# Half-width transposes without a copy ahead of them, a reordered first batch, and channel products placed between theta products, in a windowed attention with a phase-mixing layer

## The chip, the cores and the metric

The kernel runs on one core of a Trainium2 chip. The metric is the device time of one execution in microseconds, measured over several runs. A core has a matrix engine (PE; its weight loads are listed as PEld), a vector engine (DVE, VectorE), an activation engine (ACT, ScalarE), a general engine (POOL, GpSimd), a synchronisation engine (SP) and sixteen DMA engines. Each engine works through its own instructions in order; SP, ACT and POOL also issue transfers.

## The reference

Four batches, eight heads of 64, 768 tokens, float32. First an attention in which a token sees the 96 tokens up to itself and the first 8 tokens, with a bias that falls with distance:

```python
scores = scale * np.matmul(q, k.transpose(0, 1, 3, 2))
is_global = pos[None, :] < int(n_global)              # 8
is_local = (rel >= 0) & (rel < int(n_local))          # 96
bias = -slopes[:, None, None] * dist[None, :, :]
a = softmax(np.where(is_global | is_local, scores + bias, -1e9))
x = np.matmul(a, v)                                   # heads side by side: 768 x 512
```

Then a layer in which tokens are mixed by two 768 x 768 matrices:

```python
theta = x @ w_theta
zr, zi = x * np.cos(theta), x * np.sin(theta)
u = x + w_tok_r @ zr + w_tok_i @ zi
out = u + np.maximum(u @ w_ch, 0.0)
```

## The kernel before

Tokens are tiled by 128, so a batch has NT = 6 token tiles; channels by 128, NC = 4; heads go in NP = 4 pairs, one pair filling 128 partitions with two heads of 64. Matrix work is in bf16.

**Loads.** POOL's queue loads and converts everything but the first head pair of batch 0, which comes as float32 through SP and ACT (L99) and is converted by the engines. `load_qk` (L70) gives each partition p the six consecutive tokens 6p to 6p+5 of each head; `load_v` (L86) has tokens by tile. The order on POOL is: Q and K of batch 0's pair 1, V's first half, pairs 2 and 3, V's second half, the weights (`load_w`, L154), then Q, K and V of batch 1, Q and K of batch 2, and later the rest.

**Transposed Q and K.** The scores need Q and K with the head dimension on partitions. For batches 0, 1 and 2 VectorE first copies a pair of heads from the loaded layout (head, token, 64) into `qkn`, laid out (token, head, 64): `cast0` (L193) for batch 0, `prep_copy` (L224) for batches 1 and 2. Then PE transposes six blocks of 128 x 128 into a PSUM tile (`turn0` L200, `prep` L232), and an engine copies the tile to `qT` or `kT` (`out0` L206; L249 on VectorE, L251 on ScalarE). `kglob` (L214) builds `kG`, K's tiles with their first 8 columns replaced by the 8 global tokens. Batch 3 is transposed by DMA instead (`prep_dma`, L256).

**Attention.** For a pair and a chunk of two key tiles, `score_mms` (L279) fills a PSUM tile: a matmul has 64 rows, and the two heads lie in the two halves of the rows. `score_exp` (L298) is one exponential on ScalarE. In batch 0 the bias is added by a matmul with a scaled identity (`score_bias`, L270); in the others VectorE multiplies by a table `etab` that ScalarE makes (`bias_table`, L140). `vglob` (L325) builds V's counterpart of kG, `values` (L336) multiplies by V and normalises into `x_sb`, and `xtrans` (L364) transposes a pair of x, by PE in batch 0 and by DMA later.

**The layer.** `theta` (L378) takes two token tiles; it has two steps, j = 0 (channel tiles 0 to 2 of the first token tile) and j = 1 (the rest, then cos and sin on ScalarE, L395, and the products zri on VectorE, L398). Channel tile 3 comes last, since it needs the last head pair. `mix` (L403) is the token mixing, `utrans` (L418) transposes u, `chan` (L430) makes the channel product, the output tile `o_sb` (L440) and its store (L442). `trans_w` (L164) transposes the mixing matrices.

**Order.** Batch 0's attention and theta are in an order written out by hand, from L510 to L574: three pairs are in flight, transposes are two pairs ahead, values one behind. From L580 on, `weave` (L488) traces the mixing of batch b as main work, with the preparation and attention of batch b+1 and the preparation of b+2 woven in by weights, and a scheduler settles each engine's final order. Before the mixing of batch b stand its theta steps `th` and the last three channel products of the batch before, `rest`, in the order of L587:

```python
order = th[:4] + rest[:2] + th[4:] + rest[2:] if b else []
```

PSUM has two large tiles, for scores, values and theta, and four small ones (`ps_small`) for all else.

Of the kernel before, what the change touches and what calls it, by code (L numbers as in the profile page):

```python
# [9 lines left out]
FP = mybir.dt.float32  # L10
# [6 lines left out]
def kernel(  # L17
# [13 lines left out]
    nc = tc.nc  # L31
# [76 lines left out]
    load_qk(0, 2, 2)  # L108
    load_v(0, 0, 4)
    load_qk(0, 4, 2)  # L110
# [29 lines left out]
    def bias_table(p):  # L140
        for h in (2 * p, 2 * p + 1):
            nc.scalar.activation(etab[:, h], dist[:, 0:5], AF.Exp, scale=-slopes[h])
# [50 lines left out]
    def cast0(p, i_, eng, h=None):  # L193
        if (p, "n") not in tiles0:
            tiles0[p, "n"] = att.tile([T, NT, 2, 2, D], BF, name="qkn", bufs=2)
        src = qk32[:, i_] if p == 0 else loads[0][0][:, i_, 2 * p:2 * p + 2]
        hs = slice(0, 2) if h is None else slice(h, h + 1)
        eng(out=tiles0[p, "n"][:, :, i_, hs].rearrange("p t h d -> p h t d"), in_=src[:, hs])

    def turn0(p, i_):  # L200
        qkn = tiles0[p, "n"]
        ps = tiles0[p, i_] = ps_small([T, NT, T], BF)
        for t_ in range(NT):
            nc.tensor.transpose(ps[:, t_, :], qkn[:, t_, i_].rearrange("p h d -> p (h d)"), ident)
# [9 lines left out]
    def kglob(b, p):  # L214
        kT = qkT[(b, p)][1]
        kG = qkT[(b, p)][2] = att.tile([T, NT - 2, T], BF, name="kG", bufs=6)
        with behind("dve") if b == B - 1 else nullcontext():
            nc.vector.tensor_copy(
                out=kG, in_=kT[:, T:(NT - 1) * T].rearrange("p (t n) -> p t n", t=NT - 2))
            nc.vector.tensor_copy(out=kG[:, :, 0:NG], in_=kT[:, None, 0:NG].to_broadcast([T, NT - 2, NG]))  # L220

    qkns = {}

    def prep_copy(b, p):  # L224
        qk = loads[b][0]
        qkn = qkns[b, p] = att.tile([T, NT, 2, 2, D], BF, name="qkn", bufs=2)
        with behind("dve"):
            for i_ in range(2):
                nc.vector.tensor_copy(  # L229
                    out=qkn[:, :, i_].rearrange("p t h d -> p h t d"), in_=qk[:, i_, 2 * p:2 * p + 2])  # L230

    def prep(b, p):  # L232
        if p == 0:
            prep_copy(b, 0)
        if p + 1 < NP:
            prep_copy(b, p + 1)
        qkn = qkns[b, p]
        qT = att.tile([T, S], BF, name="qT", bufs=6)
        kT = att.tile([T, S], BF, name="kT", bufs=6)
        for i_, dst in ((0, qT), (1, kT)):  # L240
            ps = ps_small([T, NT, T], BF)
            with behind("pe"):
                for t_ in range(NT):
                    nc.tensor.transpose(ps[:, t_, :], qkn[:, t_, i_].rearrange("p h d -> p (h d)"), ident)  # L244

            dst = dst.rearrange("p (n t) -> p n t", t=NT)
            src = ps.rearrange("p t n -> p n t")
            if i_ == 0:
                nc.vector.tensor_copy(out=dst, in_=src)  # L249
            else:  # L250
                nc.scalar.copy(out=dst, in_=src)  # L251

        qkT[(b, p)] = [qT, kT, None]
        kglob(b, p)
# [42 lines left out]

    def score_exp(b, p, c):  # L298
        e_t, pb = ebuf[(b, p)], pbs[b, p, c]
        n = min(4, 2 * NT - 1 - 4 * c) * T  # L300
        e_c = e_t[:, :, 2 * c:2 * c + 2].rearrange("p a j s n -> p a (j s n)")[:, :, 0:n]
        ins = nc.scalar.activation(e_c, pb[:, :, 0:n], AF.Exp, scale=scale).ins  # L302
        if c == NT // 2 - 1 and p == NP - 1:

            with tc.issue_after(ins) if b else nullcontext():
                nc.scalar.activation(junk, halfpi, AF.Sin)
        if b == 0:
            return
        tab = etab[:, 2 * p:2 * p + 2]
        if c == 0 or n < 4 * T:  # L310
            s0 = 0 if c == 0 else 2
            nc.vector.tensor_mul(e_c, e_c, tab[:, :, s0:s0 + n // T].rearrange("p a s n -> p a (s n)"))  # L312
        else:
            e4 = e_t[:, :, 2 * c:2 * c + 2].rearrange("p a j s n -> p a j (s n)")
            nc.vector.tensor_mul(  # L315
                e4, e4, tab[:, :, 2:4].rearrange("p a s n -> p a (s n)")[:, :, None, :].to_broadcast(
                    [T, 2, 2, 2 * T]))
# [18 lines left out]
    def values(b, p, hh):  # L336
        vn = loads[b][1]
        e_t, vG = ebuf[(b, p)], vGs[b]
        h = 2 * p + hh
        if b == 0:  # L340
            po = ps_small([T, 1, 512], FP)
        else:
            if hh == 0:
                pos[(b, p)] = ps_big()
            po = pos[(b, p)][:, hh:hh + 1, :]
        for it in range(NT):
            mms = [(e_t[:, hh, it, 0, :], vn[:, h, it, :])]
            if it:
                mms.append((e_t[:, hh, it - 1, 1, :], vG[:, h, it - 2, :] if it > 1 else vn[:, h, 0, :]))
            o = po[:, 0, it * (D + 1):(it + 1) * (D + 1)]  # L350
            for i_, (l_, r_) in enumerate(mms):
                nc.tensor.matmul(o, lhsT=l_, rhs=r_, start=(i_ == 0), stop=(i_ == len(mms) - 1))  # L352
        if b and hh == 0:
            return
        if b:
            po = pos[(b, p)]
        h0, n = (hh, 1) if b == 0 else (0, 2)
        po4 = po[:, :, 0:NT * (D + 1)].rearrange("p a (t d) -> p a t d", d=D + 1)
        rec = att.tile([T, n, NT, 1], FP, name="rec", tag=f"rec{n}")
        nc.vector.reciprocal(rec, po4[:, :, :, D:D + 1])  # L360
        xv = x_sb[b][:, p, :, h0 * D:(h0 + n) * D].rearrange("p t (a d) -> p a t d", a=n)
        nc.vector.tensor_mul(xv, po4[:, :, :, 0:D], rec.to_broadcast([T, n, NT, D]))  # L362

    def xtrans(b, p, copy=nc.vector.tensor_copy):  # L364
# [6 lines left out]
        for st in range(NT):  # L371
            nc.tensor.transpose(ps[:, st * T:(st + 1) * T], x_sb[b][:, p, st, :], ident)
        copy(out=xT_sb[b][:, p, :], in_=ps)
# [4 lines left out]
    def theta(b, c, j):  # L378
        if c == 0 and j == 0:
# [3 lines left out]
        if j == 0:  # L383
            pss["th"] = [ps_small([T, DM], FP) for _ in range(2)] if last else ps_big()
        pb = pss["th"]
        st = lambda j_: slice((2 * c + j_) * T, (2 * c + j_ + 1) * T)
        for j_, dc in ([(0, dc) for dc in range(NC - 1)] if j == 0 else
                       [(1, dc) for dc in range(NC - 1)] + [(0, NC - 1), (1, NC - 1)]):
            nc.tensor.matmul(pb[j_] if last else pb[:, j_, :], lhsT=xT[:, dc, st(j_)],  # L389
                             rhs=w_theta_bf[:, dc, :], start=(dc == 0), stop=(dc == NC - 1))  # L390
        if j == 1:
# [26 lines left out]
    def utrans(b, tt):  # L418
# [3 lines left out]
        if b and (b, tt) != (B - 1, NT - 1):  # L422
# [7 lines left out]
    def chan(b, tt):  # L430
        u, uT = u_sb[b, tt], uTs[(b, tt)]
        ps_c = ps_small([T, DM], FP)
        for dc in range(NC):
            nc.tensor.matmul(ps_c, lhsT=uT[:, dc, :], rhs=w_ch_bf[:, dc, :],  # L434
                             start=(dc == 0), stop=(dc == NC - 1))
        o_sb = moe.tile([T, DM], FP, name="o_sb", bufs=4)
        parts = 2 if (b, tt) == (B - 1, NT - 1) else 1
        for i_ in range(parts):
            cols = slice(i_ * DM // parts, (i_ + 1) * DM // parts)
            nc.vector.scalar_tensor_tensor(o_sb[:, cols], in0=ps_c[:, cols], scalar=0.0, in1=u[:, cols],  # L440
# [72 lines left out]
    cast0(0, 1, dve, 0)  # L513
    cast0(0, 1, act, 1)
    turn0(0, 1)
    cast0(0, 0, dve, 0)
    cast0(0, 0, act, 1)
    turn0(0, 0)
    out0(0, 1, act, 0)
# [3 lines left out]
    kglob(0, 0)  # L523
    score_bias(0, 0)
    score_bias(0, 1)
    score_mms(0, 0, 0)
    score_mms(0, 0, 1)
    score_exp(0, 0, 0)
    cast0(1, 1, dve)
    cast0(1, 0, dve)  # L530
    diagonals(1)
    turn0(1, 1)
    turn0(1, 0)
    for p in range(NP):
        nxt = p + 1 < NP
        score_exp(0, p, 1)
        if nxt:
            out0(p + 1, 1, act)
            out0(p + 1, 0, dve)
            kglob(0, p + 1)  # L540
# [3 lines left out]
        score_bias(p, 2)  # L544
        score_mms(0, p, 2)
        score_exp(0, p, 2)
        if p + 2 < NP:
            cast0(p + 2, 1, dve)
            cast0(p + 2, 0, dve)
            diagonals(p + 2)  # L550
        if p == 0:
            vglob(0, 0, 4)
        if p == 1:
            vglob(0, 4, 4)
        if nxt:
            score_bias(p + 1, 0)
            score_mms(0, p + 1, 0)
            score_exp(0, p + 1, 0)
            score_bias(p + 1, 1)
            score_mms(0, p + 1, 1)  # L560
            if p + 2 < NP:
                turn0(p + 2, 1)
                turn0(p + 2, 0)
        if p:
            xtrans(0, p - 1, act if p == NP - 1 else dve)
    values(0, NP - 1, 0)
    values(0, NP - 1, 1)
    trans_w(0, nc.scalar.copy)
    xtrans(0, NP - 1)
    for c in range(NT // 2):  # L570
        theta(0, c, 0)
        theta(0, c, 1)
    for p in range(NP):
        bias_table(p)  # L574
# [5 lines left out]
    for b in range(B):  # L580
# [6 lines left out]
        order = th[:4] + rest[:2] + th[4:] + rest[2:] if b else []  # L587
# [72 lines left out]
```

The softmax here doesn't subtract the row's maximum and nothing guards it: scores larger than these inputs give would overflow.

## Time and profile before

| what | time |
|---|---|
| four runs | 174.58, 174.95, 174.95, 176.87 us; median 174.95 |
| the profiled execution | 174.52 us, of which the span shown is 172.6 us |
| PE busy | 159.4 us (92%), 1457 matmuls |
| VectorE busy | 128.0 us (74%), 288 instructions |
| ScalarE busy | 99.1 us (57%), 124 instructions |
| transfers | 25.92 MB, 150 GB/s over the span |

The profile is one execution. A line of a group names the source line, the engine, the operation and its tiles as output <- inputs, with the partitions and elements of each; a tile's name is that of the program. A line of the timeline begins with the start and the length in us; several instructions that follow each other are merged (x6), and a bracket gives the idle time of the engine before it and what ended that. Matmuls overlap in the pipe, so the distance from one start to the next tells more than their duration. The chain of waits is followed back from the last instruction. Its last steps before are the tail of the kernel:

```profile
166.99 0.32 PE ps L427 x4
167.31 1.74 PE ps L434 x8
169.07 0.42 DVE o_sb L440
169.50 0.33 DVEq L655
```

### The profile page before, as it was taken

What the parts mean: (1) busy time and instruction counts of PE and PEld (TensorE: products, weight loads), DVE (VectorE), ACT (ScalarE), POOL (GpSimd) and SP (SyncE); (2) the same over time, 40 slices, a digit from 0 to 9 for tenths busy, and PEclk for the clock granted to TensorE, in tenths of its full rate; (3) what the DMA queues carried; (4) which work ended last, traced back from release to release, by engine and by line L of the source; (5) the groups of instructions that cost most, each with busy time, mean ns of one, the idle gap of its engine ahead of it and who ended that gap; (6) DMA issues with size and microseconds to landing.
All of it is one profiled execution on the core that took longest, in us unless ns stands there. A gap on an engine that the chain in (4) does not pass through costs nothing.

```text
span 172.6 us, 3627 instructions
## 1 busy us (share of the span) xinstructions
PE 159.4 (92%) x1457; PEld 84.3 (49%) x1482; DVE 128.0 (74%) x288; ACT 99.1 (57%) x124; POOL 37.3 (22%) x45
## 2 busy tenths in 40 slices
PE   6779978999999999999999998999999989999991
PEld 1345655455756566544454463444554634444440
DVE  7578965677999999999587588597786837724443
ACT  2479676999497595489834740989348308500010
POOL 8983346005272010099100000000000000000000
PEclk9999999999999999999999999999999999999999
DMA  4999999999999999799999697787138471323335
GB/s 152 190 195 178 210 208 209 204 204 169 162 204 173 166 155 165 103 105 164 209 127 133 157 158 167 137 153 223 30 76 132 116 168 43 143 40 102 101 93 182
DMA packets 75088, 25.92 MB, mean 150 GB/s; under 512 B 63168, under 2 KB 72128, under 8 KB 75072
## 3 DMA queue, kind: packets, MB, share of 16 engines
q0 software_dynamic: 45680, 12.45, 79.1%
q1 hardware_dynamic: 28976, 12.72, 34.6%
q10 hardware_dynamic: 416, 0.52, 0.9%
q8 instruction: 11, 0.18, 0.4%
q14 instruction: 5, 0.04, 0.1%
HBM read 25.69 MB, written 6.29 MB: 185 GB/s over the span
## 4 chain that ended last, share of the span: by engine, by line
PE 49%; DMA 22%; DVE 19%; POOL 5%; issue 2%; ACT 1%; SPq 0%; DVEq 0%; POOLq 0%
PE ps L409 27%; DMA qk<-in_k_dram 11%; PE ps L434 9%; DMA w_nat<-in_moe_w_tok_r_dram 7%; PE pb L295 4%; PE pb L352 3%; PE pb L389 3%; DVE qT L249 3%; POOL qk L73 3%; DVE e L312 2%; DVE qkn L229 2%; PE ps L389 2%; DVE o_sb L440 2%; POOL vn L88 2%; DMA kT<-qk 2%
## 5 line engine op out<-in xcount | busy, mean ns | idle before, releaser
L409 PE MATMUL ps<-zri,w_tokT 128*128 128x512 bf16 x271 | 67.4, 379 | 1.5 <-issue 0.5
L302 ACT ACTIVATE e<-pb 128x1024 bf16<-128x1024 f32 (+1 forms) x48 | 43.6, 958 | 22.6 <-PE pb L295 22.4
L409 PEld LDWEIGHTS <-w_tokT 128*128 128x128 bf16 x288 | 26.1, 98 | 29.0 <-issue 1.0
L414 DVE TENSOR_TENSOR u<-x_sb,ps 128x512 bf16<-128x512 bf16 x24 | 16.4, 682 | 14.6 <-PE ps L409 12.7
L434 PE MATMUL ps<-w_ch_bf,uT 128*128 128x512 bf16 x94 | 23.9, 379 | 0.3 <-DVE u L414 0.2
L398 DVE TENSOR_TENSOR zri<-x_sb,cs 128x512 bf16<-128x512 bf16 x48 | 17.9, 418 | 7.8 <-ACT cs L395 7.5
L440 DVE SCALAR_TENSOR_TENSOR o_sb<-ps,u 128x512 f32<-128x512 f32 (+1 forms) x25 | 16.5, 662 | 3.1 <-PE ps L434 3.1
L395 ACT ACTIVATE cs<-pb,halfpi 128x1024 bf16<-128x1024 f32 x8 | 8.9, 1115 | 15.6 <-PE pb L389 15.6
L312 DVE TENSOR_TENSOR e<-e,etab 128x1024 bf16<-128x1024 bf16 (+1 forms) x24 | 14.7, 615 | 3.5 <-ACT e L302 3.5
L295 PE MATMUL pb<-qT,kT 64*128 64x128 bf16 x224 | 15.7, 221 | 0.8 <-ACT kT L211 0.3
L389 PE MATMUL pb<-w_theta_bf,xT 128*128 128x512 bf16 x62 | 15.0, 379 | 1.1 <-DMA xT<-x_sb 1.0
L295 PEld LDWEIGHTS <-kT 64*128 64x128 bf16 x224 | 9.0, 94 | 14.2 <-issue 13.0
L389 PEld LDWEIGHTS <-xT 128*128 128x128 bf16 x96 | 9.1, 98 | 11.9 <-DMA xT<-x_sb 2.2
L428 ACT COPY uT<-ps 128x512 bf16<-128x512 bf16 x7 | 4.1, 587 | 18.6 <-PE ps L427 18.6
L352 PEld LDWEIGHTS <-e 128*128 128x128 bf16 x352 | 12.7, 97 | 3.0 <-issue 1.0
L434 PEld LDWEIGHTS <-uT 128*128 128x128 bf16 x96 | 8.8, 98 | 10.2 <-DMA uT<-u 0.4
L88 POOL DMA_DIRECT2D vn<-in_v_dram x5 | 9.6, 1923 | 11.8 <-DVE vn L68 10.2
L295 PE MATMUL pb<-qT,kG 64*128 64x128 bf16 x128 | 11.7, 217 | 0.3 <-DVE kG L220 0.3
L362 DVE TENSOR_TENSOR x_sb<-pb,rec 128x768 bf16<-128x768 f32 x12 | 11.4, 949 | 0.3
L315 DVE TENSOR_TENSOR e<-e,etab 128x1024 bf16<-128x1024 bf16 x12 | 8.2, 684 | 2.8 <-ACT e L302 2.8
L352 PE MATMUL pb<-vn,e 128*128 128x65 bf16 x168 | 9.6, 193 | 0.2
L251 ACT COPY kT<-ps 128x768 bf16<-128x768 bf16 x8 | 6.4, 798 | 5.1 <-PE ps L244 5.1
(74 smaller groups left out, 204.9 us busy)
## 6 DMA issues: line engine op xcount, KB each, us to landing
out_dram<-o_sb SPq DMA_DIRECT2D x23, 256.0 KB, 2.4
vn<-in_v_dram POOLq DMA_DIRECT2D x3, 768.0 KB, 22.6
qk<-in_q_dram POOLq DMA_DIRECT2D x2, 768.0 KB, 20.7
qk<-in_k_dram POOLq DMA_DIRECT2D x2, 768.0 KB, 23.2
w_nat<-in_moe_w_tok_r_dram POOLq DMA_DIRECT2D x3, 384.0 KB, 14.2
w_nat<-in_moe_w_tok_i_dram POOLq DMA_DIRECT2D x3, 384.0 KB, 15.4
vn<-in_v_dram POOLq DMA_DIRECT2D x2, 384.0 KB, 8.7
qk<-in_q_dram POOLq DMA_DIRECT2D x8, 96.0 KB, 9.1
```

The lines of the kernel that those rows point to most:

```text
L88: nc.gpsimd.dma_start(out=vn[:, h0:h0 + n, :, 0:D].rearrange("p h t d -> p (h t) d"), in_=v[b, h0:h0 + n].rearrange("h (t p) d -> p (h t) ...
L295: nc.tensor.matmul(pb[:, hh, o:o + T], lhsT=lhsT, rhs=qT[R, (own, nxt)[part]], start=bool(b), stop=bool(b) or (jt == NT - 1 or (j == 1 and ...
L302: ins = nc.scalar.activation(e_c, pb[:, :, 0:n], AF.Exp, scale=scale).ins
L312: nc.vector.tensor_mul(e_c, e_c, tab[:, :, s0:s0 + n // T].rearrange("p a s n -> p a (s n)"))
L352: nc.tensor.matmul(o, lhsT=l_, rhs=r_, start=(i_ == 0), stop=(i_ == len(mms) - 1))
L362: nc.vector.tensor_mul(xv, po4[:, :, :, 0:D], rec.to_broadcast([T, n, NT, D]))
L389: nc.tensor.matmul(pb[j_] if last else pb[:, j_, :], lhsT=xT[:, dc, st(j_)], rhs=w_theta_bf[:, dc, :], start=(dc == 0), stop=(dc == NC - 1))
L398: nc.vector.tensor_mul(zri[b][:, i_, 2 * c + j_, :].rearrange("p (g d) -> p g d", g=NP), xb[:, :, 2 * c + j_, :], cs[:, i_, j_].rearrange( ...
L409: anchor["pe"] = nc.tensor.matmul(ps, lhsT=w_tokT[wi][:, st, tt * T:(tt + 1) * T], rhs=zri[b][:, wi, st, :], start=(st == 0 and wi == 0), ...
L414: anchor["dve"] = nc.vector.tensor_add(u_sb[b, tt].rearrange("p (g d) -> p g d", g=NP), x_sb[b][:, :, tt, :], ps.rearrange("p (g d) -> p g ...
L434: nc.tensor.matmul(ps_c, lhsT=uT[:, dc, :], rhs=w_ch_bf[:, dc, :], start=(dc == 0), stop=(dc == NC - 1))
L440: nc.vector.scalar_tensor_tensor(o_sb[:, cols], in0=ps_c[:, cols], scalar=0.0, in1=u[:, cols], op0=ALU.max, op1=ALU.add)
```

## The change

Five things change.

1. Q and K are transposed straight from the loaded layout. A block of 128 tokens by one head's 64 columns is transposed into one half of the PSUM tile's partitions, so that a pair's tile takes twelve transposes of 64 columns in place of six of 128. The copies `prep_copy` are gone, and `cast0` remains only for the float32 pair 0, now contiguous.
2. Batch 0's hand-written order is another one: bias products of pair 0 ahead of its transposes, one bias table made at the start, kG of pair 0 in two pieces on ScalarE, values and x transposes at other places, the last pair's values in two pieces of four and two token tiles, and theta of the channel tiles of pairs 0 to 2 ahead of the last pair's x.
3. On POOL, Q and K of pair 2 are loaded ahead of V's first half.
4. Of the channel products `rest`, the first now stands behind the first theta step and the second behind the fourth.
5. The very last channel product is made as two of 256 columns, each with its own PSUM tile, vector step and store.

```diff
-    load_v(0, 0, 4)
     load_qk(0, 4, 2)
+    load_v(0, 0, 4)
...
-    def cast0(p, i_, eng, h=None):
...
-    def turn0(p, i_):
-        qkn = tiles0[p, "n"]
-        ps = tiles0[p, i_] = ps_small([T, NT, T], BF)
-        for t_ in range(NT):
-            nc.tensor.transpose(ps[:, t_, :], qkn[:, t_, i_].rearrange("p h d -> p (h d)"), ident)
+    qk0 = att.tile([T, 2, 2, NT, D], BF, name="qk0", bufs=1)
+    def cast0(i_, eng, h):
+        eng(out=qk0[:, i_, h], in_=qk32[:, i_, h])
+    def turn(ps, src):
+        for t_ in range(NT):
+            for hh in range(2):
+                nc.tensor.transpose(ps[hh * D:(hh + 1) * D, t_, :], src[:, hh, t_, :], ident)
+    def turn0(p, i_):
+        ps = tiles0[p, i_] = ps_small([T, NT, T], BF)
+        turn(ps, loads[0][0][:, i_, 2 * p:2 * p + 2] if p else qk0[:, i_])
...
-    def prep_copy(b, p):
...
-        qkn = qkns[b, p]
...
             with behind("pe"):
-                for t_ in range(NT):
-                    nc.tensor.transpose(ps[:, t_, :], qkn[:, t_, i_].rearrange("p h d -> p (h d)"), ident)
+                turn(ps, qk[:, i_, 2 * p:2 * p + 2])
...
     def theta(b, c, j):
-        if c == 0 and j == 0:
+        last0 = [(j_, NC - 1) for j_ in range(2)]
+        part = {0: [(0, dc) for dc in range(NC - 1)],
+                1: [(1, dc) for dc in range(NC - 1)] + last0,
+                2: [(j_, dc) for j_ in range(2) for dc in range(NC - 1)],
+                3: last0}[j]
...
     def chan(b, tt):
-        ps_c = ps_small([T, DM], FP)
-        for dc in range(NC):
-            nc.tensor.matmul(ps_c, lhsT=uT[:, dc, :], rhs=w_ch_bf[:, dc, :],
-                             start=(dc == 0), stop=(dc == NC - 1))
+        parts = 2 if (b, tt) == (B - 1, NT - 1) else 1
+        n = DM // parts
+        pss_c = [ps_small([T, n], FP) for _ in range(parts)]
+        for i_, ps_c in enumerate(pss_c):
+            for dc in range(NC):
+                nc.tensor.matmul(ps_c, lhsT=uT[:, dc, :], rhs=w_ch_bf[:, dc, i_ * n:(i_ + 1) * n],
+                                 start=(dc == 0), stop=(dc == NC - 1))
...
+    score_bias(0, 0)
+    score_bias(0, 1)
+    cast0(1, dve, 0)
+    bias_table(0)
+    cast0(1, act, 1)
     turn0(0, 1)
...
+    kglob(0, 0, 0, 1, act)
     score_mms(0, 0, 0)
+    kglob(0, 0, 1, NT - 2, act)
     score_exp(0, 0, 0)
...
+    score_exp(0, p, 2)
+    sine_table()
+    xtrans(0, p - 1, dve)
+    values(0, p, 0, 0, 4)
+    values(0, p, 1, 0, 4)
+    trans_w(0, act)
+    theta(0, 0, 2)
+    xtrans(0, p, dve, 0, 4)
+    values(0, p, 0, 4, 6)
+    values(0, p, 1, 4, 6)
+    theta(0, 1, 2)
+    xtrans(0, p, dve, 4, 6)
+    theta(0, 0, 3)
+    theta(0, 1, 3)
+    theta(0, 2, 2)
+    theta(0, 2, 3)
+    for h in range(1, H):
+        bias_table(h)
...
-        order = th[:4] + rest[:2] + th[4:] + rest[2:] if b else []
+        order = th[:1] + rest[:1] + th[1:4] + rest[1:2] + th[4:] + rest[2:] if b else []
```

The function `utrans` also gets a condition for token tiles from 6 up, of which there are none.

## The prediction

> **What bounds the kernel now.** I read the page first, then the chain of waits by time, then busy time by stretches, then the timeline where the chain changes engine. Page and chain:
>
> ```profile
> PE 159.4 (92%) x1457; PEld 84.3 (49%) x1482; DVE 128.0 (74%) x288; ACT 99.1 (57%) x124; POOL 37.3 (22%) x45
> DMA  4999999999999999799999697787138471323335
> ...
> PE ps L409 27%; DMA qk<-in_k_dram 11%; PE ps L434 9%; DMA w_nat<-in_moe_w_tok_r_dram 7%; PE pb L295 4%; PE pb L352 3%; PE pb L389 3%; DVE qT L249 3%; POOL qk L73 3%; DVE e L312 2%; DVE qkn L229 2%; PE ps L389 2%; DVE o_sb L440 2%; POOL vn L88 2%; DMA kT<-qk 2%
> ```
>
> ```profile
> 9.39 12.63 DMA w_nat<-in_moe_w_tok_r_dram
> 22.02 0.28 issue
> 22.31 19.42 DMA qk<-in_k_dram
> 41.73 0.02 issue
> 41.75 0.52 DVE qkn L229 x2
> ```
>
> Three stages. **Stage A, to 41.7 us:** the transfer stream. The DMA line stands at 9 to beyond 60 us; K of batch 1 is issued at 22.31 and lands 19.42 us later. **Stage B, 41.7 to about 72 us** (rest of batch 0's token mixing, batch 1's attention, transposes for batches 1 and 2): VectorE, as the stretches show (us; busy time and instructions of PE, PEld, DVE, ACT, POOL; clock; DMA):
>
> ```profile
> 50.00:55.00 5.00, 4.97 (x73) 2.94 (x71) 5.00 (x10) 4.00 (x5) 1.52 (x2) 1.00 1.73 188
> 55.00:60.00 5.00, 4.66 (x63) 2.49 (x57) 5.00 (x11) 3.33 (x4) 0.82 (x1) 1.00 3.08 165
> 60.00:65.00 5.00, 4.51 (x75) 3.27 (x77) 5.00 (x13) 4.43 (x5) 0.83 (x1) 1.00 2.09 155
> ```
>
> VectorE is busy all of each stretch; PE's 4.5 to 5.0 is not full work, since its matmuls overlap. **Stage C, from 72 us:** PE. Its largest stalls are at the batch changes, where theta (L389) waits for the last pair's transposed x:
>
> ```profile
> 139.39 1.46 PE L389 MATMUL pb<-w_theta_bf,xT 128*128 128x512 bf16 x6
> ...
> 141.35 2.33 PE L389 MATMUL pb<-w_theta_bf,xT 128*128 128x512 bf16 x9 [0.50 <-DMA xT<-x_sb]
> ...
> 143.52 1.89 PE L434 MATMUL ps<-w_ch_bf,uT 128*128 128x512 bf16 x8
> ```
>
> A 512-column matmul passes every 0.216 us (1.89 = 7 steps + one duration of 0.379). Six end at 139.39 + 1.30 = 140.69, so 0.66 us is lost before 141.35; at 105.40 the same gives 106.70 to 107.34, 0.64. The channel products (L434) that could fill it stand behind.
>
> **What the Trainium skill says.** "TensorEngine Tiling (Array Packing)", Key Properties: different tiles can execute weight loads and matmuls in parallel, but changing the tiling mode drains the engine. The trace agrees for row tiles: L295's 64-row pairs start 57 ns apart, two matmuls each (81.36, 81.42, 81.48, 81.53), though one lasts 0.22 us; entering and leaving costs about 0.1 us (16 between 81.19 and 81.74, 0.55 against 16 x 0.028 = 0.45). The same page, Restrictions: column tiling disables Fast Weight Load. No run here has a narrow weight load. "TensorE: Matmul & The Clock Gate", LDWEIGHTS: about P/1.2 ns for P columns, so an estimate of 64/1.2 = 53 ns for a half-width load; the trace's full loads already repeat at 30 ns in L352 (14.52, 14.55, 14.58), so here that formula is only an upper bound.
>
> **The change, part by part.** Times are against the profiled execution: span 172.6, its own time 174.52 (1.9 around the span), 0.43 under the median 174.95 of four.
>
> *1. Copies removed.* L229 goes: 16 copies in stage B, 0.27 us from start to start where they follow each other (chain: 43.52, 43.98, 45.40; single durations below). 16 x 0.27 = 4.3 us off the engine that bounds B. In batch 0 (L198), six copies of 0.34 to 0.37 us go and four casts become contiguous; that is under stage A's transfers: nothing by itself.
>
> ```profile
> L229 DVE COPY qkn<-qk x16: 283/346/360, 41.3 to 70.2; 128x768 bf16<-128x768 bf16 x16
> 13.71 0.84 PE L204 MATMUL ps<-ident,qkn 128*128 128x128 bf16 x12
> ```
>
> *2. Transposes doubled.* 144 of full width become 288 of half width. Now they pass every (0.84 - 0.22)/11 = 56 ns. Let p be the new pace. Ends: 28 ns if the column halves run side by side like L295's row halves, 56 ns if one stream of weights or matmuls serves both, 107 ns if load and matmul (53 + 54) don't overlap. A gain below 28 is excluded: L295 shows two per 56 ns as the moving time of 128 columns. I take 31, two tiles in parallel with the drains spread over them. From 41.7 to 72.1 PE's work by pace is 43 mixing + 12 channel + 1 theta matmuls (56 x 0.216 = 12.1), 88 scores (x 0.0345 = 3.0), 88 values (x 0.030 = 2.7), 48 other transposes (2.7) and 96 of these (x 0.056 = 5.4): 25.9 us in 30.4. After: 20.5 + 192p; p = 31 gives 26.5, p = 56 gives 31.3. VectorE's need becomes 30.4 - 4.3 = 26.1. The two are level and wait for each other (scores, ScalarE's exponentials at 0.93, multiply, values), so I add 1.3: 27.8. **Stage B: -2.6.**
>
> What else could be late in B: V of batch 1 lands at 24.77 + 23.2 = 47.97; VectorE in its new order reaches vG (L333 before) at about 48.2, by its list from 43.2: just covered. K of batch 2 lands at 27.99 + 27.0 = 55.0, its transposes come near 58: covered. The transposes now wait for the load on PE itself, with mixing queued behind: at 41.7 PE arrives when K does in both kernels.
>
> *3. Batch 0's new order* (loads of pair 2 ahead of V, bias products and the first bias table early, kG in pieces on ScalarE, theta of pairs 0 to 2 ahead of pair 3, Sin's table right behind the last exponential). On POOL, V's first half is passed by two issues (0.70 + 0.75) and two transfers, landing about 1.5 us later than the 10.8 at which POOL's wait for it ended; its use at 13.3 has room. On ScalarE kG costs four copies, about 1.1 us (an estimate: L211's 0.48 for 384 columns, and three of about 0.2, like the one-column activation of L306), in place of 0.9 on VectorE (8.06, 8.82). Theta's 24 matmuls now begin before the last pair's x is transposed: of PE's waits near 25 us (0.78 and 0.30) about 1 us goes, and removed copies give perhaps another 0.5. But mixing before the transposes stays 28 matmuls, 24 transposes of weights and four of u (28 x 0.216 + 28 x 0.056 = 7.6), so PE then stands before K of batch 1, whose landing is set by bytes ahead of it, the same bytes. **Stage A: 0**, bounds -0.5 (the stream slips forward) to +1 (batch 0 slower than its cover of about 1.5).
>
> *4. Channel products between thetas.* Four matmuls (0.86) go into gaps of 0.64 and 0.66; their uT landed earlier (transposes issued at 103.24 take 2.4). Batch 1's theta has no such gap (2 then 13 matmuls at 72.12 to 75.7): there the sines start 0.86 later relative to PE, and ScalarE is on the chain at 85.25 (`ACT e L302`), so I charge +0.2, bounds 0 and +0.8. The vector step and store of these products move forward with them on VectorE and SP; SP's list keeps its order. **-0.6 - 0.6 + 0.2 = -1.0.**
>
> *5. Last tile by halves.* Eight matmuls of 256 columns for four of 512: equal streaming. The first half's vector step (half of 169.07's 0.76) and store run under the second half's products. **-0.35**, bounds 0 and -0.5.
>
> Sum: -2.6 + 0 - 1.0 - 0.35 = -3.95: 170.6 for the profiled execution, 171.0 for the median.
>
> **The rivals.**
>
> *R1, half-width transposes don't pair (p about 50 to 56).* For it: no fast weight load. Against it: L295's pairs. At 56 stage B is PE-bound at 31.3, +0.9; batch 0's 48 extra (2.7) exceed its cover by about 1; less 1.35: near 175.5. At 45 it gives 29.1 + 0.5 in B: about 173. So 173 to 175.5.
>
> *R2, slower: load and matmul serialize in the half-width tiles (p of 75 and more).* At 80, stage B is 20.5 + 15.4 = 35.9, +5.5; batch 0 adds 96 x 0.080 - 48 x 0.056 = 5.0, of which 1.5 is covered, +3.5; less 1.35: about 182.5. It decides from the pace at which 192p - 9.9 passes 3.1 us with stage A's excess: p near 58 is 1% slower.
>
> *R3, B is held by something that the copies don't touch* (V's landing at 47.97, four small PSUM buffers, the exponentials): gain of B near 1, total 172.5. For it: all four transposes of batch 1 now stand ahead of its first scores; the list by pace from 41.7 puts the first exponential at 47.6, where it was. Against it: VectorE was busy without a break.
>
> *R4, what was hidden by transfers pays after all* or VectorE and PE fit perfectly: 168.5 to 169.5.
>
> **How the numbers follow.** A change of 1% (1.75 us) is about what a measurement of this kernel tells from none. The forecast (170 to 172) 0.45, R3 0.13, R4 0.10, R1 0.22 (a third of it under 173.2), R2 0.10. Faster: 0.45 + 0.13 + 0.10 + 0.04 = 0.72; slower: 0.10 and a fifth of R1, 0.14; the rest same, 0.14. The range 168.4 to 175.4 leaves out R2 and the ends of R4 and R1; where faster cases hold, their own range is 168.4 to 173.
>
> **What would show it.** Right: no copies in front of the transposes; the transposes of a stretch starting in pairs about 57 ns apart; PE idle for a microsecond or more before K of batch 1 at 41.7; theta of the last batch starting without the 0.66 us stall. Wrong: half-width transposes at 50 ns or more each, or their loads lengthened; K's landing moved by over 1 us; VectorE waiting for V near 48; the chain after 42 us on PE's transposes.

## The result, and the profile after

The changed kernel takes **175.21 us** (median of 36 runs, 174.52 to 177.01) against 174.93 for the kernel before (55 runs): ratio **1.003, interval 1.0015 to 1.0045**. Forecast were 171.0 us and a gain. The profiled execution spans 173.2 us (before 172.6).

The profile page of the changed kernel: busy time by engine, the transfer engines over 40 slices, and the shares of the chain that ended last.

```profile
PE 159.1 (92%) x1604; PEld 84.2 (49%) x1630; DVE 123.6 (71%) x270; ACT 99.4 (57%) x127; POOL 38.3 (22%) x45
...
DMA  4999999999999999989999697797345373313335
...
PE 53%; DVE 17%; ACT 11%; DMA 11%; POOL 4%; issue 2%; DVEq 0%; SPq 0%; ACTq 0%; POOLq 0%
PE ps L403 26%; PE ps L431 7%; DMA vn<-in_v_dram 7%; ACT cs L389 6%; PE pb L383 5%; PE pb L281 4%; ACT e L291 3%; PE pb L340 3%; DMA xT<-x_sb 3%; POOL qk L73 3%; DVE x_sb L351 2%; PE ps L200 2%; DVE e L300 2%; PE ps L383 2%; DMA kT<-qk 2%
```

VectorE's busy time fell by 4.4 us (128.0 to 123.6), yet the span grew. By places in the two traces: the first transposes of batch 1 start at 42.12 (before 41.69), theta of batch 1 at 73.22 (72.12), theta of batch 2 at 106.59 (105.40), the end is at 173.2 (172.6). So stage A lost 0.4, stage B 0.7 in place of a gain of 2.6, and stage C gave 0.5 back. Stage A's end is no longer the landing of batch 1's K, as it was before. K lands at 42.08, but the chain runs through batch 0's sines, which start at 30.61 (before 29.91), and then through TensorE's own list without a pause:

```profile
40.46 1.73 PE ps L403 x8
42.19 0.79 PE ps L200 x24
```

The stretches of stage B that the prediction showed, in the changed kernel (same columns):

```profile
50.00:55.00 5.00, 4.62 (x70) 2.87 (x70) 5.00 (x10) 4.25 (x6) 3.79 (x4) 1.00 1.67 188
55.00:60.00 5.00, 4.55 (x75) 2.78 (x73) 4.94 (x11) 2.98 (x4) 0.82 (x1) 1.00 2.53 173
60.00:65.00 5.00, 4.95 (x85) 3.26 (x85) 4.80 (x11) 4.83 (x6) 0.83 (x1) 1.00 2.32 151
```

VectorE is still busy nearly all of the time, though the copies into `qkn` are gone. Busy time isn't need: the same kG piece of 32 columns takes 0.08 us at 47.02 in the changed kernel's chain and 0.38 at 50.45, and counts as busy all the while.

The transposes, the first group of batch 0 in the timeline, and theta of batch 3 with the channel product between its parts:

```profile
6.00 0.86 PE L200 MATMUL ps<-ident,qk 128*64 128x128 bf16 x24 [0.36 <-DVE qk L195]
```

```profile
140.05 0.59 PE L383 MATMUL pb<-w_theta_bf,xT 128*128 128x512 bf16 x2
141.01 0.39 PE L383 MATMUL pb<-w_theta_bf,xT 128*128 128x512 bf16 x1 [0.37 <-DMA xT<-x_sb]
141.24 1.03 PE L431 MATMUL ps<-w_ch_bf,uT 128*128 128x512 bf16 x4
142.10 2.97 PE L383 MATMUL pb<-w_theta_bf,xT 128*128 128x512 bf16 x12
```

Twenty-four half-width transposes take about as long as twelve full ones did, (0.86 - 0.22)/23 = **28 ns** each: the column halves pair fully. In the second fence the product stands where it was meant to, but theta now waits ahead of it, at 141.01, for an x transpose that took 4.4 us instead of 2.8; that comes back below.

### The profile page after: what moved, and what is told of

Same layout as the page of the kernel before. It is cut to its first block, busy times and chain, and to the rows that moved or that the text cites. A ratio compares the mean times of both kernels' runs of the same rounds, so it can differ in the third digit from the quotient of the medians.

```text
span 173.2 us, 3902 instructions
## 1 busy us (share of the span) xinstructions
PE 159.1 (92%) x1604; PEld 84.2 (49%) x1630; DVE 123.6 (71%) x270; ACT 99.4 (57%) x127; POOL 38.3 (22%) x45
## 4 chain that ended last, share of the span: by engine, by line
PE 53%; DVE 17%; ACT 11%; DMA 11%; POOL 4%; issue 2%; DVEq 0%; SPq 0%; ACTq 0%; POOLq 0%
PE ps L403 26%; PE ps L431 7%; DMA vn<-in_v_dram 7%; ACT cs L389 6%; PE pb L383 5%; PE pb L281 4%; ACT e L291 3%; PE pb L340 3%; DMA xT<-x_sb 3%; POOL qk L73 3%; DVE x_sb L351 2%; PE ps L200 2%; DVE e L300 2%; PE ps L383 2%; DMA kT<-qk 2%
## 5 line engine op out<-in xcount | busy, mean ns | idle before, releaser
L403 PE MATMUL ps<-zri,w_tokT 128*128 128x512 bf16 x272 | 68.3, 379 | 2.2 <-DVE zri L392 0.7
L431 PE MATMUL ps<-w_ch_bf,uT 128*128 128x512 bf16 (+1 forms) x96 | 24.3, 371 | 0.2
L281 PE MATMUL pb<-qT,kT 64*128 64x128 bf16 x224 | 15.2, 219 | 3.0 <-DVE qT L211 1.4
L200 PE MATMUL ps<-ident,qk 128*64 128x128 bf16 x288 | 10.8, 221 | 0.6 <-DVE qk L195 0.4
L200 PEld LDWEIGHTS <-qk 128*64 128x64 bf16 x288 | 8.7, 109 | 4.4 <-issue 2.5
```

The lines of the kernel that those rows point to most:

```text
L200: nc.tensor.transpose(ps[hh * D:(hh + 1) * D, t_, :], src[:, hh, t_, :], ident)
L281: nc.tensor.matmul(pb[:, hh, o:o + T], lhsT=lhsT, rhs=qT[R, (own, nxt)[part]], start=bool(b), stop=bool(b) or (jt == NT - 1 or (j == 1 and ...
L403: anchor["pe"] = nc.tensor.matmul(ps, lhsT=w_tokT[wi][:, st, tt * T:(tt + 1) * T], rhs=zri[b][:, wi, st, :], start=(st == 0 and wi == 0), ...
```

## The experiments

Each is timed against the kernel before on the same chip. The first four put one part of the change into the kernel before.

**x1_transposes: the half-width transposes of batches 1 and 2 alone.**

```diff
-        if p == 0:
-            prep_copy(b, 0)
-        if p + 1 < NP:
-            prep_copy(b, p + 1)
...
-                for t_ in range(NT):
-                    nc.tensor.transpose(ps[:, t_, :], qkn[:, t_, i_].rearrange("p h d -> p (h d)"), ident)
+                turn(ps, qk[:, i_, 2 * p:2 * p + 2])
```

> The kernel before with the half-width transposes straight from the loaded q and k in batches 1 and 2, without the sixteen copies; batch 0, the channel products and the last tile as before. Theory (stage B itself lost: all four preparations of batch 1 stand ahead of its first scores and the copies had filled VectorE's gaps): no gain, +0.3 to +1.2 us, ratio 1.002 to 1.007, and batch 1's first theta matmul 30.9 to 31.5 us after the first transposes of batch 1 instead of 30.4. Rival A (stage B would have gained, but batch 0's new order hands it its work late): -1.5 to -2.6 us, ratio 0.985 to 0.991.

Measured: 175.09 against 174.71 us, 1.0023 (1.0003 to 1.0043). As the theory said: no gain, 0.4 us lost; rival A falls. Its stage B has the changed kernel's order of instructions, and lasts from 41.29 to 72.66, 31.4 us (before 30.4). This difference is larger than the spread of the traces: five with half-width transposes and the full mixing (x1, z2, the changed kernel, w3, w4) have 31.1 to 31.4. At its start VectorE stands where the copies ran before: it waits for TensorE's transposes, then for a copy of K by ScalarE, which works on the bias table until 42.29:

```profile
41.86 0.96 DVE L238 COPY qT<-ps 128x768 bf16<-128x768 bf16 x1 [0.64 <-PE ps L225]
43.49 0.29 DVE L218 COPY kG<-kT 128x512 bf16<-128x512 bf16 x1 [0.67 <-ACT kT L240]
```

**x2_products: the channel products between the thetas alone**, and **x2b_products_late**, which leaves batch 1's order as it was.

```diff
-        order = th[:4] + rest[:2] + th[4:] + rest[2:] if b else []
+        order = th[:1] + rest[:1] + th[1:4] + rest[1:2] + th[4:] + rest[2:] if b else []
```

> The kernel before with the channel products between the thetas alone. Theory: the two stalls of 0.65 us of batches 2 and 3 go and batch 1's transition pays 0.2 to 0.6, so -0.7 to -1.1 us, ratio 0.994 to 0.996. Rival (ScalarE's sines come later by the four matmuls and stand on the chain in every transition): -0.3 to +0.3 us, ratio 0.998 to 1.002.

> The kernel before with the channel products between the thetas in batches 2 and 3 alone; batch 1 keeps its old order. In x2_products TensorE waited 0.38 us for ScalarE's exponential at 85.75, as it does not in the kernel before. Theory (the later sines of batch 1 cost what the forecast charged, 0.2 us, up to 0.4): -0.1 to -0.4 us against x2_products, ratio to before 0.992 to 0.9945. Rival (nothing is lost at batch 1, since TensorE's list ends later anyway): within 0.1 us of x2_products.

Measured: x2 173.66 us, **0.9942** (0.9923 to 0.9960), 1.0 us gained; x2b 173.54, **0.9924** (0.9899 to 0.9949). Both beat both kernels. The two can't be told from each other by their intervals. In x2b TensorE no longer waits for the exponential near 85 (0.2 us in x2's waits), but 0.5 us for a transposed u. Theta of batch 3 in x2 runs without a gap:

```profile
139.33 0.81 PE L389 MATMUL pb<-w_theta_bf,xT 128*128 128x512 bf16 x3
139.98 1.03 PE L434 MATMUL ps<-w_ch_bf,uT 128*128 128x512 bf16 x4
140.84 2.97 PE L389 MATMUL pb<-w_theta_bf,xT 128*128 128x512 bf16 x13
```

Three products (single matmul instructions) of theta start at 139.33, the four of the channel follow 0.65 us later, and theta goes on 0.86 = 4 x 0.216 after that: the 0.66 us stall of the kernel before is filled.

**x3_batch0: batch 0's new order alone.** The diff is the change's own, without `prep`, the order above and the last tile; the cast of pair 0 shares the buffer of the copies, which stay.

> The kernel before with batch 0's new order alone (half-width transposes in batch 0, loads of pair 2 ahead of V, last pair by token pieces with theta of the other pairs ahead); batches 1 and 2 prepared with copies as before. The cast of pair 0 shares the buffer of the copies. Theory (the sines of batch 0 start 0.7 us later and the mixing behind them waits): +0.3 to +0.7 us, ratio 1.002 to 1.004. Rival A (batch 0's order is what spoils stage B): +1.5 us or more, ratio over 1.008. Forecast: 0.

Measured: 176.19 us, 1.007 (1.0049 to 1.0092): 1.2 us lost, more than the theory gave and short of rival A.

**x4_tail: the last tile by halves alone.**

> The kernel before with the last tile's product by two halves of 256 columns alone. Forecast: -0.35 us. Theory from the trace of after (the last store is issued 0.27 us sooner and lands 0.3 us later after its issue): -0.1 to +0.1 us.

Measured: 174.87 us, 1.0003 (0.9981 to 1.0024). No gain, as the theory said. In the last 13 us of the changed kernel and of the kernel before (transfers: bytes, median us to landing):

```profile
out_dram<-o_sb ACTq DMA_DIRECT2D x1, 128.0 KB, 2.1
```

```profile
out_dram<-o_sb ACTq DMA_DIRECT2D x1, 128.0 KB, 1.8
```

From the start of the last two tiles' products (167.67, before 167.14) to the issue of the last store the halves save 0.27 us (2.45 against 2.72), and the store lands 0.3 us later after its issue. x4's own trace has the same 2.45 and 2.1. The interval, 0.4 us to either side, ends about where the forecast lies.

The four ratios multiply to 1.004; the whole change measured 1.003. So the parts add up, and two questions remain: why x1 gains nothing, and why x3 loses 1.2.

**Why the copies' removal gains nothing.** The start of stage B in x1, TensorE's timeline:

```profile
41.29 0.86 PE L225 MATMUL ps<-ident,qk 128*64 128x128 bf16 x24
42.09 1.04 PE L398 MATMUL ps<-zri,w_tokT 128*128 128x512 bf16 x4
43.05 1.20 PE L225 MATMUL ps<-ident,qk 128*64 128x128 bf16 x36
44.18 0.39 PE L398 MATMUL ps<-zri,w_tokT 128*128 128x512 bf16 x1
```

The last of the 24 transposes starts at 41.29 + 0.64 = 41.93, the next product 0.16 later instead of 0.028. The last of the four products starts at 42.75, the next transpose 0.30 later instead of 0.216. So each change of tile shape costs 0.09 to 0.13, about 0.11 us, whichever way. I take it for the drain which the Trainium skill ("TensorEngine Tiling (Array Packing)", Key Properties) names without a price. Counted over stage B with each kind's own pace, and VectorE's need as about the smallest step of each form, from start to start, times its count:

| | TensorE's matmuls | changes of shape | other waits of TensorE | VectorE's need |
|---|---|---|---|---|
| before, 31.0 us | 25.7 | 26: 2.9 | 2.4 | 29.6 |
| x1, 31.7 us | 25.7 | 35: 3.9 | 2.1 | 27.4 |

(The matmuls of before include 1.3 us for six of the mixing that the trace lacks: it has 37, x2b's, x3's and x4's have 43; the sums begin a product or two ahead of the first transposes, so they are 0.3 to 0.6 us over the stage. The copies are taken at 0.24 us; of fifteen, two took 0.21 and the others 0.27. VectorE's 27.4 include 1.3 us, a q copy and a pair of kG copies above all, that in the kernel before stand outside the stage.) VectorE's need did fall, by 3.5 us like for like, and TensorE's 25.7 + 3.9 = **29.6 us is about what VectorE needed before**. By these sums the larger need changed its engine and kept its size. The chain agrees in part: before, 27.3 of stage B's 30.4 us lie on VectorE and 3.0 on TensorE; in x1 16.7 lie on VectorE, 11.3 on TensorE and 3.2 on ScalarE, and from 65.6 on TensorE holds it alone. The next experiments test this account.

**x7_full_direct: no copies, and no half-width transposes either.** Heads and tokens stand in another order than in the reference.

```diff
+                    flat = qk[:, i_, 2 * p:2 * p + 2].rearrange("p h t d -> p (h t d)")
+                    nc.tensor.transpose(ps[:, t_, :], flat[:, t_ * T:(t_ + 1) * T], ident)
```

> The kernel before with the sixteen copies of batches 1 and 2 left out and the transposes kept at full width, six per tile: each takes 128 consecutive columns of the loaded q or k, so that heads and tokens stand in another order than in the reference. It differs from x1_transposes in the width of the transposes alone. Account of TensorE in stage B, from the traces: before, 25.7 us of matmuls by their pace + 26 changes of tile shape x 0.11 = 2.9 + stalls 2.3 = 30.9; x1, 25.7 + 35 x 0.11 = 3.9 + 2.1 = 31.4 to 31.7. Theory (TensorE's in-order stream with its changes of shape bounds stage B beside VectorE): here 25.7 + 2.0 (18 changes, the scores') + 2.1 = 29.8, so -0.7 to -1.5 us against before and about -1.0 to -1.9 against x1; ratio 0.991 to 0.996. Rival (VectorE's copies alone bounded the stage, and only the half-width form spoils it): -2.6 us or more, ratio under 0.986.

Measured: 174.67 us, 0.9987 (0.9967 to 1.0007): 0.2 us, less than the theory's 0.7. The rival, VectorE's copies as the only bound, is out by 2.4 us. By the account TensorE needs 25.8 + 20 changes of shape, 2.2, that is 1.6 us less than in x1; of this 1.2 us came in the trace (stage B 41.14 to 71.32, 30.2 us), and TensorE's other waits grew to 2.8. So with the copies gone and six changes of shape fewer than before, stage B is still only 0.2 us shorter than before: the waits of the engines for each other are as large a term as the changes. In x7 theta, just begun, also stands 0.3 us at 72.07 for a transposed x that took 7.8 us.

**x8_less_mixing and x9_both: 2.6 us less for TensorE, with the copies and without.** Both leave out the twelve imaginary products of two token mixings.

```diff
-            for wi in range(2):
+            n = 1 if b == 0 and tt in (3, 4) else 2
+            for wi in range(n):
```

> The kernel before without the twelve imaginary products of two of batch 0's token mixings (tiles 3 and 4), that is 12 x 0.216 = 2.6 us off TensorE in stage B; the sixteen copies stay. Theory of two bounds side by side (VectorE needs about 29.6 of the 30.9 us by its own durations, TensorE 28.6): -0.3 to -1.3 us. Rival A (TensorE alone bounds): -2.2 us or more. Rival B (VectorE alone bounds): -0.3 to +0.3 us.

> x1_transposes (half-width, no copies in batches 1 and 2) without the same twelve mixing products. Theory: with the copies gone TensorE is the bound, so that its 2.6 us come off nearly whole: -2.0 to -2.6 us against x1_transposes, -1.6 to -2.3 us against before, more than x1 and x8 give each by itself together. Rival (a chain of dependences through scores, exponentials, products and values holds stage B, not one engine): no more than -1.0 us against before.

Measured: x8 176.41 us, 1.012 (1.0077 to 1.0163), **slower** by 1.6; outside all three expectations. x9 173.95, 0.9954 (0.9935 to 0.9972): 0.8 us under before and 1.1 under x1: short of the theory (2.0) and inside what the rival allows (at most 1.0 under before). x8's chain shows one thing that happened:

```profile
59.95 8.47 DMA xT<-x_sb
68.42 0.05 issue
68.47 0.39 PE pb L389
```

With less mixing to place, the scheduler set two of theta's products (one in the kernel before) ahead of the last transposes in TensorE's order, and TensorE stood 1.9 us for the second pair's transposed x, which takes 8.5 us here among batch 3's loads. So x8 doesn't test the two bounds. In x9 the new order brought 40 changes of shape in place of x1's 35, so that TensorE's relief is 2.6 less 0.55, about 2.0 us. Stage B itself takes 29.7 us there (41.53 to 71.23) and 31.4 in x1: 1.7 of the 2.0 arrived, and some 0.5 was lost again behind it. So the stage follows TensorE's sum, by about three quarters of its change from x1 to x7 and more from x1 to x9; but the total, which was forecast, is the rival's.

**z2_x1_late_loads and z4_x9_late_loads: is it that landing?** The first eight of batch 3's q and k loads move behind batch 1's x.

```diff
-            side.append((0, lambda: (alloc_qk(3), load_qk_tokens(3, 0, H // 2))))
+            side.append((0, lambda: alloc_qk(3)))
-            load_qk_tokens(b, H // 2, H // 2)
+            load_qk_tokens(b, 0, H)
```

> x1_transposes with the first eight of batch 3's sixteen q and k loads moved behind batch 1's last transposed x, to the other eight, so that they no longer share the transfer engines with batch 1's x transposes. In x1 the third pair's transposed x was issued at 65.12 and landed at 71.25 (6.1 us; 2.7 us in later batches), in the changed kernel 65.68 to 73.20, just ahead of theta at 73.2. Theory (three limits stand close together in stage B: VectorE's list, TensorE's list, and this landing; in x1 TensorE is the last of them): x's third transposes take about 3 to 4 us, but theta starts no more than 0.5 us earlier; -0.5 to +0.5 us against x1. Rival (the landing behind batch 3's loads is what holds stage B once the copies are gone): -1.5 us or more against x1.

> x9_both (no copies, twelve mixing products left out) with batch 3's loads moved in the same way. In x9 TensorE was relieved of 2.6 us, but theta of batch 1 still began at 71.4, just behind the landing of the third pair's transposed x at 71.18. Theory (with VectorE and TensorE relieved the landing is the limit): theta begins at 69.0 to 70.2, so -1.0 to -2.0 us against x9 unless the moved loads delay stage C. Rival (a chain of dependences through scores and values holds it): theta within 0.4 us of 71.4.

The transposes of x between 60 and 76 us, in x1 and then in z2:

```profile
DMA to landing us min/median/max: 3.0/6.1/8.5
```

```profile
DMA to landing us min/median/max: 2.7/2.8/4.1
```

The landing came 3.5 us sooner, and theta of batch 1 started at 72.56 instead of 72.66. So in x1 it holds nothing; TensorE's own list stands ahead of theta there. In z4 the third pair landed at 67.0 instead of 71.2, but theta started at 70.80 against 71.23: 0.4 us, not the theory's 1.2 or more, and z4's stage B had begun 0.37 us sooner too: it lasts 29.6 us against 29.7. So the landing isn't the limit there either. x9's chain has TensorE's own list without a break from 61.8 us to theta, and ahead of that goes to and fro between the engines (of the stage TensorE 13.4, VectorE 12.9, ScalarE 3.5 us); the rival's chain through scores, exponentials and values isn't shown apart from this. (Both lose in total, 1.0114 and 1.0052, a loss that z2's forecasts had not and z4's named as possible: V of batch 3 lands at 98 us instead of 92 or 93, in stage C.)

**x6_scores_sooner**, on x1, emits the third and fourth preparation behind batch 1's first scores, for R3's reason.

> x1_transposes with the third and fourth preparation of batch 1 emitted behind its first scores in place of ahead of them. Theory (the order with all four ahead costs little, since the engines' sums bound the stage): within 0.5 us of x1. Rival R3's reason (all four preparations ahead of the first scores hold batch 1's attention back): first exponential about 1.4 us sooner and -0.8 to -1.4 us against x1.

Measured: 182.42 us, 1.0441 (1.0406 to 1.0475). It doesn't test the reason, since the scheduler now put V's copy ahead of the q copies. VectorE's timeline:

```profile
47.35 0.71 DVE L322 COPY vG<-vn 128x2080 bf16<-128x2080 bf16 x1 [6.16 <-DMA vn<-in_v_dram]
48.09 0.70 DVE L323 COPY vG<-vn 8x2080 bf16<-8x2080 bf16 x1
48.72 0.94 DVE L238 COPY qT<-ps 128x768 bf16<-128x768 bf16 x1
```

VectorE stands 6.2 us for V, all of batch 1's q copies stand behind it, and TensorE's scores behind those (5.7 us). It is the accident that the prediction named for V's landing, at 47.3.

**Why batch 0's order costs 1.2 us.** Two edits of x3: **y1_v_order** puts V's first half back ahead of pair 2; **y2_sines_first** completes theta of the first token pair ahead of the second.

```diff
-    theta(0, 1, 2)
-    xtrans(0, p, dve, 4, 6)
-    theta(0, 0, 3)
+    theta(0, 0, 3)
+    theta(0, 1, 2)
+    xtrans(0, p, dve, 4, 6)
```

> x3_batch0 (batch 0's new order alone) with the loads in their old order, V's first half ahead of pair 2. Theory (in the new load order V's second half lands at 17.4 to 18.6 instead of 17.05, and the POOL queue, which waits for these landings before it issues w_ch and batch 1's q and k, hands everything on late): -0.5 to -1.0 us against x3, within 0.6 us of before. Rival (the order of batch 0's compute is what costs): no change against x3, +0.9 to +1.5 us against before.

> x3_batch0 with theta of the first token pair completed (its two products with the last pair) ahead of the twelve... that is: theta(0,0,3) right after the last pair's first token piece is transposed, and ahead of theta(0,1,2). Theory (stage A lost because the first sines waited for theta of the second token pair: sines from 30.27 instead of 29.91): the sines start at 28.9 to 29.6, and the time falls by 0.5 to 1.0 us against x3_batch0, to -0.2 to +0.7 against before. Rival (stage A is set by something ahead of the sines, or by batch 1's landing): no change against x3_batch0, +1.0 to +1.4 against before.

Measured: y1 176.40 us, 1.009 (1.0066 to 1.0115); y2 176.27, 1.0084 (1.0057 to 1.0111). No change against x3, so both theories fall. The granted clock isn't the cause: nine of x3's runs had a mean clock of 0.986 to 0.990 and a median of 176.21 us, the other thirteen (0.996 to 1.000) one of 176.16. The traces say where to look: theta of batch 2 starts at 105.71, 105.33 and 105.67 in x3, y1 and y2 (before 105.40), but they end at 173.5, 174.5 and 174.3 (172.6). Most of the loss lies in stage C, where the program is the same. Two steps of the chain at batch 3's k transposes, in the kernel before and in y1, and y1's queues between 107.8 and 110.6 us (packets, MB, share):

```profile
107.82 2.77 DMA kT<-qk
```

```profile
107.76 4.03 DMA kT<-qk
```

```profile
q8 instruction: 1, 0.02, 2.9%
```

The transpose that batch 3's kG waits for, with zri behind it on VectorE, took 1.3 us longer, and in that time one packet of instructions came, 16 KB in about 1 us. The kernel before has none there. Such packets come 11 to 13 times on this queue, one to about 120 of TensorE's matmuls on record (63 to 178 apart), so I take them for the fetches of TensorE's program. In the traces of before, after, y1 and x3, 16 of the 19 transposes of 3.8 to 4.6 us in stage C have one inside them; those that a packet met near their start or end took 2.5 to 3.8. In the changed kernel one falls into the last pairs' x transposes, whose chain is `136.58 4.39 DMA xT<-x_sb`. If this is so, instructions added on TensorE move all later packets. Four runs change only work in idle time at the start: they add products of one column on zeros, and w2 to w4 leave out three to five of the six full ones that are there:

```diff
+        for _ in range(n):
+            nc.tensor.matmul(ps[:, 0:1], lhsT=zero[:, 0:T], rhs=zero[:, 0:1], start=True, stop=True)
```

> The kernel before with 48 products of one column on zeros at the start, behind the six that are there, where TensorE is idle from 3.9 to 5.6 us; as many instructions as batch 0's doubled transposes add. Theory (instruction fetches of TensorE's program, 16 KB every 125 or so products, stretch the DMA transposes that they meet; 48 more move the fetches of stage C from about 99, 117, 130 and 142 us to 94, 109, 126, 136 and 159, onto the k transpose that batch 3's kG waits for and the x transposes ahead of the last theta): +0.5 to +1.5 us against before, all of it behind theta of batch 2. Rival (they lie in idle time, and batch 0's order itself costs what x3 measured): -0.2 to +0.2 us.

> x3_batch0 with the six products at the start replaced by one of them and 80 of one column, 75 more. Theory: with 48 + 75 = 123 more than before the fetches are back near 100, 117, 129 and 143 us, so -0.6 to -1.4 us against x3, within 0.5 us of before. Rival (batch 0's order costs it): no change against x3, +0.9 to +1.5 us against before.

> The changed kernel with 48 products of one column in place of three of the six at the start, 45 more. In its trace a fetch at 139.0 met the third pair's x transposes ahead of the last theta (4.4 us, and theta then waited 0.53). Theory: the fetches come near 108, 125, 135 and 162 us instead, the last theta's wait goes, and the time falls by 0.3 to 0.8 us against the changed kernel. Rival: no change (-0.2 to +0.2).

> The changed kernel with one of the six products at the start and 100 of one column, 95 more, which ends some 0.5 us later than the six did, ahead of the first transposes. Theory: fetches near 102, 121, 130 and 151 us, none on a transpose that theta or kG waits for: -0.3 to -1.0 us against the changed kernel. Rival: no change (-0.2 to +0.3).

| run | us | ratio to before (interval) | theta of batch 2, end in the trace |
|---|---|---|---|
| before | 174.80 | | 105.40, 172.6 |
| w1 | 175.41 | 1.0027 (1.0000 to 1.0053) | 105.92, 173.5 |
| w2 | 176.16 | 1.0069 (1.0046 to 1.0093) | 106.99, 174.3 |
| w3 | 175.34 | 1.0021 (0.9993 to 1.0049) | 106.92, 173.2 |
| w4 | 174.88 | 0.9984 (0.9959 to 1.0008) | 106.50, 172.5 |

The packets came where they were forecast, within 3 us but for the last of w3 and w4 (6 us): in w1 at 94.3, 108.9, 124.3, 136.2 and 159.3 us. w1 is slower by 0.6, on the lower edge of what was expected, and over half of it (0.5 of 0.9 in the trace) comes ahead of theta of batch 2, where none was expected: TensorE waits 0.7 us at 93.87 for a transposed u that took 3.9 us with a packet inside it. Batch 3's k transpose took 3.2 us, not y1's 4.0. w4 is 0.5% under the changed kernel (0.9984 against 1.003), 0.8 us, as expected; its last theta doesn't wait:

```profile
139.88 0.81 PE L388 MATMUL pb<-w_theta_bf,xT 128*128 128x512 bf16 x3
140.52 1.03 PE L436 MATMUL ps<-w_ch_bf,uT 128*128 128x512 bf16 x4
141.39 2.97 PE L388 MATMUL pb<-w_theta_bf,xT 128*128 128x512 bf16 x12
```

w3 missed and gained nothing that can be measured: its packet at 105.6 met the x transposes of batch 2 (4.3 us) in place of batch 3's. w2 missed: behind theta of batch 2 it took 67.3 us, as before does (67.2; x3 67.8), but it lost 1.1 at 94.9, waiting for a transposed u that took 9.8 us. So the place of these packets moves the time by about half a microsecond. w4 shows it with intervals that don't overlap, though it was not timed beside the changed kernel; w1's interval begins at 1.0000. That they are all of x3's 1.2 us isn't shown, and the rest stays open.

## Why the prediction was wrong, point by point

- **Copies removed.** Right in itself: VectorE's need in stage B fell by 3.5 us (3.9 with the copies at their usual 0.27); fifteen copies stood inside it, not sixteen. It is 27.4 in x1, not 26.1, since a q copy and a pair of kG copies now fall into the stage. What failed is the next step.
- **Transposes doubled, and the sum for stage B.** The pace was forecast at 31 ns and is 28; R1 and R2 fall with it. That R1's times (173 to 175.5) and the end of the stated range, set by them, hold the measured 175.21 is luck. **The step that failed is "After: 20.5 + 192p; p = 31 gives 26.5".** This sum counts matmuls by their pace alone. The drains, from the Trainium skill, were named, even measured at "about 0.1 us" for entering and leaving, and then not multiplied. That reading was also half of what it should be: 81.19 to 81.74 holds the leaving alone, and the first score starts 0.31 us after the product ahead of it (80.88, by the pace from 80.23) instead of 0.216. Counted in full, 26 changes were in the stage already and nine came, 3.9 us, where spreading drains over p had charged 192 x 3 ns = 0.6. TensorE's need was 29.6, not 26.5. The 1.3 for mutual waits was small too (2.1 in x1, 2.8 in x7), and x7 shows that without the added changes of shape the gain would still have been near 0.2 us, not 2.6.
- **R3** (something that the copies don't touch) came nearest in its reason, and was given 0.13; its gain near 1 in stage B and 172.5 us did not come either. Of its reasons, V's landing is refuted: it came at 48.30, and VectorE reached vG at 49.8. Exponentials show as TensorE waits of 0.2 to 0.3 us and as 1.0 us of stage B's chain in x1 and the changed kernel, but as 6.5 in z2; the PSUM buffers weren't tried. Nor is the order with all preparations first settled, since x6 was lost to another wait. The argument against R3, "VectorE was busy without a break", was true and no argument: TensorE was nearly as close to its own limit (25.7 + 2.9 = 28.6 against 29.6).
- **V and K landings.** Covered, as forecast. But TensorE was to stand for a microsecond or more before K of batch 1; it came to the transposes at 42.12, as K landed (42.08, before 41.73), without a pause. The cover of batch 0's order was used up, and stage A's 0.4 us in the changed kernel is that.
- **Batch 0's new order, 0 with bounds -0.5 to +1.** The time to theta of batch 2 agrees (0 to +0.3 in x3, y1, y2). The measured 1.2 is past the upper bound. Missing was a way by which it could act 60 us later; the instruction packets are one, and how much of the 1.2 is theirs is open.
- **Channel products between thetas, -1.0.** Measured -1.0 (x2). The charge at batch 1 can't be separated (x2b). In the changed kernel the last theta stalls again, at 141.01, behind the slow x transpose.
- **Last tile by halves, -0.35.** Measured 0, to within 0.4: the store's landing took it back.

With the products' gain kept, the miss is stage B's term (+0.4 for -2.6), batch 0's (+1.2 for 0) and the tail's. (In the sum of chances a third of R1's 0.22 is 0.07, not 0.04.)

## What to carry to other kernels

Where one engine looks full, sum the next one's need too, changes of tile shape included, before pricing what its relief brings: the gain ends where the second engine's sum begins, and here 2 to 3 us of the engines' waits for each other came on top. A small edit to TensorE's program moved the time by about half a microsecond here through transfers far behind it; put the same number of idle instructions in the old kernel to see that part alone. Of a change in several parts, time each alone: here one line holds the whole gain, and the rest gave it back.

## What the runs showed of the hardware

- Half-width column tiles run in full pairs: 28 ns per transpose, though each weight load of 64 columns is on record with 106 to 110 ns. The estimate of 53 ns from the Trainium skill's load formula ("TensorE: Matmul & The Clock Gate", LDWEIGHTS) did not bind.
- A change between full, row-tiled and column-tiled matmuls costs 0.09 to 0.13 us each way, about 0.11 (x1).
- DMA transposes of 2.4 to 2.8 us mostly took 3.8 to 4.6 where a 16 KB instruction packet came well inside them; beside POOL's loads they took up to 8.5 (x1) and 9.8 (w2).
